# Zero products in TensorE's first gaps, the first pair's squares on one engine, u by tokens in single products, and two heads' sums in one tile, in a fused attention and mixer kernel

## The chip, the cores and the metric

The kernel runs on one core of one Trainium2 chip. The metric is the device time of one execution in microseconds (us), as a median of several executions. Where two kernels are compared, their runs were taken on the same chip in the same rounds.

## The reference, cut to what matters

```python
# q, k, v: (8 batches, 12 heads, 448 tokens, 64); U: (448, 32); V: (32, 448); w_ch1: (768, 3072)
q_n = q / (norm(q) + 1e-6);  k_n = k / (norm(k) + 1e-6)
attn = softmax(q_n @ k_n.T / tau)
x = (attn @ v), heads side by side        # (8, 448, 768)
u = x + (x.T @ U @ V).T                   # low rank, over tokens
out = u + relu(u @ w_ch1) @ w_ch2
```

## The kernel before

The kernel does not leave the order of instructions to the hardware or to luck. Each piece of work is an `Op` with an engine, an assumed duration, dependencies and buffers (`Slot`s of a `Ring`). A planner runs these through a list schedule and then emits them in the order of their planned starts. TensorE has several streams; at any time it takes the first stream whose next product is ready. Below that plan, the framework that the kernel is written in puts in the semaphore waits, that is, the points where one engine waits for another. A tile is a named buffer. PSUM, in the code below, is the memory into which TensorE writes its sums.

The parts that matter here:

```python
r_mm = ring(3, [128, 512], FP, "mm", psum)          # each ring entry is a PSUM tile of its own
r_sc = ring(3, [128, 512], FP, "sc", psum)
r_av = ring(2, [128, 4, D + 8], FP, "av", psum)     # sums of attn @ v, one tile for each of two heads
# ... cut ...
def attention(b, p, X):                              # one pair of heads
    # 7 score products (sc), each followed by one exponential on ScalarE (attn), then for each head
    for t in range(4):
        for j in range(4):                           # 16 products of 65 columns into av
            nc.tensor.matmul(out=av.tile[:, t, 0:D + 1], lhsT=attn..., rhs=v_t..., ...)
    # and on VectorE
    nc.vector.reciprocal(out=rd.tile, in_=av.tile[:, :, D:D + 1])                    # rd <- av
    nc.vector.tensor_mul(X.tile[...], av.tile[:, :, 0:D], rd.tile.to_broadcast(...)) # X_sb <- av, rd
# ... cut ...
def by_tokens(us, A, X):                             # batch 0: u in token order, six products
    for i in range(3):
        for c0, c1 in ((0, CH), (CH, C)):
            ...                                      # one product into mm, one addition on VectorE
# ... cut: in the first mixer product of batch 0 ...
if b == 0 and f == 9:
    by_tokens(us, *state["first"])
```

Of the kernel before, what the change touches and what calls it, by code (L numbers as in the profile page):

```python
# [10 lines left out]
FP = mybir.dt.float32  # L11
# [38 lines left out]
class Plan:  # L50
# [52 lines left out]
    def run(self):  # L103
# [22 lines left out]
        while left:  # L126
            if not events:
                raise RuntimeError("plan stuck")
            t = heapq.heappop(events)
            while events and events[0] <= t + 1e-9:  # L130
                heapq.heappop(events)
            progress = True
            while progress:
                progress = False
                for e in self.ENGINES:
                    if free[e] > t + 1e-9:
                        continue
                    pick = None
                    if e in heads:
                        for k, s in enumerate(self.streams[e]):  # L140
                            i = heads[e][k]
                            if i < len(s):
                                r = self.ready_at(s[i], e)
                                if r is None:
                                    continue
                                if r <= t + 1e-9:
                                    pick = s[i]
                                    heads[e][k] += 1
                                    break
                                heapq.heappush(events, r)  # L150
                    else:
                        w = known[e]
                        for i, (_, _, o) in enumerate(w):
                            if o.start is not None:
                                continue
                            if e == "ACT" and o.fast and free["DVE"] <= t + 1e-9:
                                continue
                            r = self.ready_at(o, e)
                            if r is None:
                                continue  # L160
                            if r <= t + 1e-9:
                                pick = o
                                break
                            heapq.heappush(events, r)
                            if r <= t + self.HOLD:
                                break
                        if pick is not None:
                            del w[i]
                    if pick is None:
                        continue  # L170
                    o = pick
                    o.start, o.by = t, e
                    o.end = t + (o.dur[e] if isinstance(o.dur, dict) else o.dur)
                    free[e] = o.end
                    o.end += self.LAG[e]
                    if isinstance(o.lat, tuple):
                        q, work, fixed = o.lat
                        dma[q] = max(dma[q], o.end) + work
                        o.end = dma[q] + fixed
                    else:  # L180
                        o.end += o.lat
                    for s in o.acq:
                        if s.i is None:
                            s.i = s.ring.n
                            s.ring.n += 1
                    for s in o.rel:
                        s.left -= 1
                        s.last = max(s.last, o.end)
                        if s.left == 0:
                            s.ring.freed[s.i] = s.last  # L190
                    for c in kids.pop(o.seq, ()):
                        waits[c.seq] -= 1
                        if waits[c.seq] == 0:
                            offer(c)
                    order.append(o)
                    left -= 1
                    progress = True
                    heapq.heappush(events, free[e])
                    heapq.heappush(events, o.end + self.SEM)
# [5 lines left out]
def kernel(  # L205
# [12 lines left out]
    nc = tc.nc  # L218
# [13 lines left out]
    EPS = 1e-6  # L232
    PE_BATCHES = 2
    LATE = 8.0

    const = ctx.enter_context(tc.tile_pool(name="const", bufs=1))
    pool = ctx.enter_context(tc.tile_pool(name="pool", bufs=1))
# [9 lines left out]
    def ring(n, shape, dt, name, space=None):  # L247
        p = space or pool
        return Ring(n, lambda i: p.tile(shape, dt, name=name, tag=name, bufs=n))
# [42 lines left out]
    r_rd = ring(2, [128, 4, 1], FP, "rd")  # L292
    r_mm = ring(3, [128, 512], FP, "mm", psum)
    r_sc = ring(3, [128, 512], FP, "sc", psum)
    r_av = ring(2, [128, 4, D + 8], FP, "av", psum)


    U_sb = const.tile([128, 2, 4, R], BF, name="U_sb")
    V_sb = const.tile([128, PAD + S + PAD], BF, name="V_sb")
    ident = const.tile([128, 128], BF, name="ident")  # L300
    w1_sb = const.tile([128, CC, F], BF, name="w1_sb")

    nc.scalar.preload_act_table_set("natural_log_exp_and_others")
# [17 lines left out]
    pe_a = plan.stream("PE")  # L321
    pe_sc = plan.stream("PE")
    pe_mlp = plan.stream("PE")
    pool_q = plan.stream("POOL")

    def pe_t(n):
        return n / 2400.0 + 0.0025
# [167 lines left out]
    def stats_first(ld, ops):  # L495

        inv = Slot(r_inv, 3)
        done, ups = {}, []
        for i in range(2):
            done[i], up = scales(0, 0, 2, ld, ops, 0, (i,), inv, -1 - 0.1 * i, ("DVE", "ACT")[i])  # L500
            ups.append(up)
        return ups + norm(0, 0, ld, 0, inv, 0, done, -1)

# [12 lines left out]
    def norm(b, p, ld, la, inv, a, deps, pr):  # L516
# [29 lines left out]
        if not by_pe:  # L546
            done = [plan.add(Op("SP", 0.1, lambda: nc.sync.dma_start_transpose(
                out=qkT.tile, in_=xn.tile.rearrange("p b e -> p (b e)")), deps=ops, acq=[qkT],
                rel=[xn], prio=0, lat=("x", 0.05 * 84, LATE)))]
        else:  # L550
            done = []
            for b0, b1, o in blocks:
                done.append(flip(
                    pe_tp, [(lambda z=z: xn.tile[:, z, :]) for z in range(b0, b1)], SCH,
                    lambda: qkT.tile, (lambda t_, x, b0=b0, b1=b1: key_tiles(t_, x, b0 // 4, b1 // 4)
                                   if b == 0 and b0 < 8 else [(t_[:, b0:b1, :], x)]),
                    [o], [qkT], [xn], 1, "ACT/DVE", 0.09 if first else 0.05, b == 0 and b0 < 8))
        got[b, p, "qkT"] = (qkT, lambda m: (done[:2] if m < 3 else done) if first else done, done)
        return ops

# [1 line left out]
    def attention(b, p, X):  # L562
# [4 lines left out]
        for m in (0, 1, 2, 6, 3, 4, 5) if b == 0 else range(7):  # L567
            sc = Slot(r_sc, 1)

            def score(sc=sc, m=m):  # L570
# [1 line left out]
                nc.tensor.matmul(out=sc.tile[:, 0:S], lhsT=kT[:, 128 * m:128 * (m + 1)],  # L572
                                 rhs=qkT.tile[:, 8:12, :].rearrange("p c s -> p (c s)"),
                                 start=True, stop=True)
            o = plan.add(Op("PE", 0.31 if b == 0 and p == 0 else pe_t(S), score, deps=qdeps(m), acq=[sc], rel=[qkT]),
                         pe_first if b == 0 else pe_sc)
            exps[m] = plan.add(Op("ACT", act_t(S), lambda sc=sc, m=m: nc.scalar.activation(  # L577
                out=attn.tile[:, m, off:off + S], in_=sc.tile[:, 0:S], func=AF.Exp,
                scale=inv_tau), deps=[o], acq=[attn], rel=[sc], prio=0.1 if b == 0 else 1))
        last_exp[b] = exps[5]  # L580
        muls = []
        for hh in range(2):
            h = 2 * p + hh
# [138 lines left out]
        prev["A"], prev["X"] = A, X  # L722
        return us, uT, ut

    def by_tokens(us, A, X):

        for i in range(3):
            for c0, c1 in ((0, CH), (CH, C)):
                mm = Slot(r_mm, 1)
                o = plan.add(Op("PE", pe_t(CH), lambda i=i, c0=c0, c1=c1, mm=mm: nc.tensor.matmul(  # L730
                    out=mm.tile[:, 0:CH], lhsT=V_sb[:, PAD + 128 * i:PAD + 128 * i + 128],
# [7 lines left out]
    def mlp(b, us, uT, ut):  # L739
# [28 lines left out]
        for f in range(NC):  # L768
            if f % AHEAD == 0:
                for g in range(f, f + AHEAD):  # L770
                    early[g] = Slot(r_sc if b == 0 and f == 0 else r_mm, 1)
                    if f == 0 and b == 0:
                        up(g, early[g], range(CC - 1))
            if b == 0 and f == 9:
                by_tokens(us, *state["first"])
            mm = early[f]
            o = up(f, mm, range(CC - 1, CC) if b == 0 and f < AHEAD else range(CC))
            r = Op("ACT/DVE", any_t(n), None, deps=[o], acq=[relu], rel=[mm],
# [65 lines left out]
        nc.vector.memset(t_[96:128, :, 0:PAD].bitcast(mybir.dt.uint32), ones)  # L844

    attn_set = [fill(lambda t_=t_: set_attn(t_), 1000, prio=i - 2.5) for i, t_ in enumerate(attn_t)]
    z = fill(lambda: nc.vector.memset(V_sb, 0.0), 500, prio=-1.3)

    def load_u(par):
        off = PAD * par  # L850
# [15 lines left out]
                       in_=V_f().rearrange("r (s c) -> r c s", c=SC))  # L866


    w2_ops = []
    NW = 4  # L870
    THIRDS = [(0, 4), (4, 8), (8, 12)]
# [4 lines left out]
    state, last_mul = {}, []  # L876

    def att(b):
        X = Slot(r_X, 0)
        muls = []  # L880
        for p in range(NPAIR):
            muls += attention(b, p, X)
        last_mul.extend(muls)
        return stage0(b, X, muls)
# [2 lines left out]
        out=lead.tile[:, i], in_=src[0, 0:2].rearrange("h (s c) d -> s h (c d)", c=SC)),  # L887
        acq=[uv], prio=-5, lat=2.5)) for i, src in enumerate((q, k))]
    second = load_qk(0, 2, 4, uses=2)
    ld, ops, _ = load_qk(0, 4, 8)  # L890
    id_set = plan.add(Op("POOL", 0.8, lambda: make_identity(nc, ident)), pool_q)
    begun = stats_first(*first[:2])
    stats(0, 2, 4, *second, hold=begun)
    xn_set.append(fill(lambda: nc.vector.memset(xn_t[2][:, 0:8, :], 0.0), 900, prio=0.2, deps=begun))
    zf = fill(lambda: nc.vector.memset(U_f(), 0.0), 400, prio=0.1, acq=[uv], deps=begun)
    u0 = load_u(0)
    v0 = [plan.add(Op("SP", 0.45, lambda t=t: nc.sync.dma_start(out=V_f()[R * t:R * (t + 1)], in_=moe_V),
                      deps=[zf, *begun], prio=-2, lat=12.0)) for t in range(4)]
    u1 = load_u(1)
    stats(0, 4, 8, ld, ops, 0, hold=got[0, 0, "qkT"][2])  # L900
    load_v0()
    ld, ops, _ = load_qk(0, 8, 12)
    late = stats(0, 8, 12, ld, ops, 0)
    load_w1(0, 6)
    load_w1(6, 12)
    v_set = [fill(lambda: set_v(v_t[0]), 1000, prio=-1.4),
             fill(lambda: set_v(v_t[1]), 1000, prio=3, deps=late)]
    consts = [plan.add(Op("POOL", 0.4, lambda: cast_u(0), deps=u0 + [z], rel=[uv]), pool_q),
              plan.add(Op("POOL", 1.2, cast_v, deps=v0 + [z], rel=[uv]), pool_q),
              plan.add(Op("POOL", 0.4, lambda: cast_u(1), deps=u1 + [z], rel=[uv]), pool_q)]  # L910
# [67 lines left out]
```

## Time and profile before

| | before |
|---|---|
| median of three executions | 604.51 us (604.49 to 605.16) |
| span of the profiled run | 603.2 us |
| TensorE busy | 586.4 us, 97% |
| full TensorE clock recorded from | 17.77 us |
| last exponential of batch 0 starts | 37.31 us |

The result below has a fourth execution of this kernel, which moves the median to 604.84.

How to read the lines further down. In the order of instructions, a line gives start, length, engine, source line, operation, output and inputs, shapes, how many were merged, and in brackets the idle time before it with what ended it. The tile names say what the work is: `sc` scores, `attn` their exponentials, `av` products with v, `rd` and `X_sb` VectorE's two steps that empty `av`, `tp` transposes, `warm` the zeros.

### The profile page before, as it was taken

Reading aid. Unit: us, or ns where it says so; the run is one execution under the profiler, and the core shown is the slowest. Engines: PE = TensorE matmul, PEld = TensorE weight load, DVE = VectorE, ACT = ScalarE, POOL = GpSimd, SP = SyncE. Lnnn points to the kernel's source line nnn. Section 1 sums busy time; section 2 is a strip of 40 time slices with the busy share of each in tenths; the row PEclk is TensorE's granted clock in tenths of the full one; section 3 lists DMA queues with packets and bytes.
Section 4 is the critical chain, followed back from the end, with each engine's and each line's share of the span. In section 5 each row is a group of like instructions: output and inputs, shape, how many; then the busy total and the mean of one; then the engine's idle time right before and its main releaser. Section 6 shows DMA issues by size and latency. Waiting matters only on the chain.

```text
span 603.2 us, 11528 instructions
## 1 busy us (share of the span) xinstructions
PE 586.4 (97%) x4725; PEld 347.0 (58%) x4725; DVE 300.6 (50%) x728; ACT 276.9 (46%) x598; POOL 115.2 (19%) x175
## 2 busy tenths in 40 slices
PE   3899999999999999999999999999999999999997
PEld 1565666555565665666445666566545666654565
DVE  8979749989999988554731244014300210110011
ACT  5877652488874277316741067505642025014300
POOL 8246334062706116000600000000000000000000
PEclk9999999999999999999999999999999999999999
DMA  9999999999999959725922133030002110310021
GB/s 144 193 188 112 204 201 107 150 173 136 159 152 155 149 102 154 95 57 90 123 29 66 52 74 47 1 93 27 15 1 53 52 40 1 90 42 1 0 53 54
DMA packets 150165, 54.81 MB, mean 91 GB/s; under 512 B 115040, under 2 KB 150112, under 8 KB 150112
## 3 DMA queue, kind: packets, MB, share of 16 engines
q0 software_dynamic: 72864, 25.73, 38.4%
q1 hardware_dynamic: 77184, 28.32, 24.4%
q8 instruction: 37, 0.61, 0.4%
q14 instruction: 16, 0.13, 0.1%
q10 hardware_dynamic: 64, 0.02, 0.0%
HBM read 52.25 MB, written 11.01 MB: 105 GB/s over the span
## 4 chain that ended last, share of the span: by engine, by line
PE 93%; DVE 2%; ACT 2%; POOL 1%; DMA 1%; issue 0%; ACTq 0%; POOLq 0%
PE mm L794 36%; PE mm L760 35%; PE sc L572 10%; PE av L592 8%; PE mm L684 1%; PE tp L374 1%; DMA v_nat<-in_v_dram 1%; DVE xn L536 1%; PE mm L649 1%; POOL v_nat L429 1%; ACT attn L577 1%; PE sc L760 0%; POOL qk_nat L396 0%; DVE ss L461 0%; ACT qkT L824 0%
## 5 line engine op out<-in xcount | busy, mean ns | idle before, releaser
L760 PE MATMUL mm<-uT,w_sb 128*128 128x512 bf16 (+1 forms) x1134 | 241.3, 353 | 0.2 <-DVE u_nat L734 0.2
L794 PE MATMUL mm<-w_sb,relu 128*128 128x384 bf16 (+1 forms) x1368 | 231.3, 323 | 0.0
L577 ACT ACTIVATE attn<-sc 128x448 bf16<-128x448 f32 x336 | 164.6, 552 | 110.9 <-PE av L592 58.2
L794 PEld LDWEIGHTS <-relu 128*128 128x128 bf16 x1368 | 132.7, 98 | 86.1 <-issue 0.2
L760 PEld LDWEIGHTS <-w_sb 128*128 128x128 bf16 x1152 | 111.8, 98 | 102.7 <-issue 1.8
L783 ACT ACTIVATE relu<-mm 128x512 bf16<-128x512 f32 (+1 forms) x158 | 86.8, 549 | 129.3 <-PE mm L760 128.7
L803 DVE TENSOR_TENSOR O_sb<-mm,u_nat 128x384 f32<-128x384 f32 (+1 forms) x57 | 31.2, 549 | 210.8 <-PE mm L794 207.4
L572 PE MATMUL sc<-qkT 128*128 128x448 bf16 x336 | 102.7, 356 | 3.7 <-ACT attn L577 2.0
L592 PEld LDWEIGHTS <-attn 128*128 128x128 bf16 x1536 | 62.1, 98 | 17.8 <-issue 2.5
L418 POOL DMA_DIRECT2D v_nat<-in_v_dram x98 | 63.2, 655 | 31.7 <-DMA w_sb<-in_moe_w_ch_dram 15.8
L592 PE MATMUL av<-v_nat,attn 128*128 128x65 bf16 x1536 | 66.6, 194 | 0.8 <-DMA v_nat<-in_v_dram 0.4
L461 DVE TENSOR_REDUCE ss<-sq 112x8 f32<-112x512 bf16 x96 | 63.1, 673 | 0.2
L536 DVE TENSOR_TENSOR xn<-qk_nat,inv 112x512 bf16<-112x512 bf16 x94 | 60.9, 681 | 2.4 <-DMA qkT<-xn 2.2
L396 POOL DMA_DIRECT2D qk_nat<-in_q_dram x24 | 17.2, 718 | 136.5 <-DVE xn L536 117.0
L572 PEld LDWEIGHTS <-qkT 128*128 128x128 bf16 x336 | 28.9, 98 | 22.1 <-issue 7.3
L601 DVE TENSOR_TENSOR X_sb<-av,rd 128x256 bf16<-128x256 f32 x96 | 40.1, 419 | 1.6
L599 DVE RECIPROCAL rd<-av 128x4 f32<-128x4 f32 x96 | 17.1, 179 | 37.6 <-PE av L592 36.9
L457 DVE TENSOR_TENSOR sq<-qk_nat 112x512 bf16<-112x512 bf16 x87 | 33.7, 415 | 0.0
L698 DVE TENSOR_TENSOR u_nat<-mm,X_sb 128x384 bf16<-128x384 f32 x36 | 19.2, 553 | 15.4 <-PE mm L684 15.1
L785 DVE TENSOR_SCALAR relu<-mm 128x384 bf16<-128x384 f32 (+1 forms) x31 | 18.7, 604 | 12.8 <-PE mm L760 12.0
L374 PE MATMUL tp<-ident,xn 112*128 112x112 bf16 x144 | 11.9, 226 | 7.8 <-DVE xn L536 7.6
L474 ACT ACTIVATE ln<-ss 112x32 f32<-112x32 f32 (+2 forms) x26 | 6.0, 231 | 27.3 <-DVE ss L461 27.1
(61 smaller groups left out, 172.5 us busy)
## 6 DMA issues: line engine op xcount, KB each, us to landing
qk_nat<-in_q_dram POOLq DMA_DIRECT2D x23, 224.0 KB, 5.2
qk_nat<-in_k_dram POOLq DMA_DIRECT2D x23, 224.0 KB, 6.3
w_sb<-in_moe_w_ch_dram POOLq DMA_DIRECT2D x4, 1152.0 KB, 14.6
w_sb<-in_moe_w_ch_dram POOLq DMA_DIRECT2D x8, 576.0 KB, 15.8
out_dram<-O_sb SPq DMA_DIRECT2D x15, 168.0 KB, 2.2
out_dram<-O_sb SPq DMA_DIRECT2D x16, 144.0 KB, 2.1
out_dram<-O_sb SPq DMA_DIRECT2D x16, 120.0 KB, 2.0
out_dram<-O_sb SPq DMA_DIRECT2D x16, 96.0 KB, 2.2
```

The costliest lines, as they stand in the source:

```text
L418: nc.gpsimd.dma_start(out=vb[p0:p0 + s1 - s0, hs, j, 0:D], in_=v[b, hs].rearrange("h (s c) d -> c s h d", c=SC)[c, s0:s1]),
L457: nc.vector.tensor_mul(y, x, x)
L461: lambda i=i, a0=a0, a1=a1, sq=sq: nc.vector.reduce_sum(ss.tile[:, i, a0:a1, :].rearrange("p h c -> p (h c)"), sq.tile[:, 0:a1 - a0, :].re ...
L536: nc.vector.tensor_mul(dst, src, sc)
L572: nc.tensor.matmul(out=sc.tile[:, 0:S], lhsT=kT[:, 128 * m:128 * (m + 1)], rhs=qkT.tile[:, 8:12, :].rearrange("p c s -> p (c s)"), start=T ...
L577: exps[m] = plan.add(Op("ACT", act_t(S), lambda sc=sc, m=m: nc.scalar.activation(out=attn.tile[:, m, off:off + S], in_=sc.tile[:, 0:S], fu ...
L592: nc.tensor.matmul(out=av.tile[:, t, 0:D + 1], lhsT=attn.tile[:, m, 128 * t:128 * (t + 1)], rhs=v_t[b % 2][:, h, j, 0:D + 1], start=(j == ...
L601: muls.append(plan.add(Op("DVE", dve_t(256), lambda av=av, rd=rd, h=h: nc.vector.tensor_mul(X.tile[:, :, h * D:(h + 1) * D], av.tile[:, :, ...
L760: o = plan.add(Op("PE", pe_t(n), lambda cc=cc: nc.tensor.matmul(out=mm.tile[:, 0:n], lhsT=w1_sb[:, cc, f * 128:(f + 1) * 128], rhs=uT.tile ...
L783: nc.scalar.activation(out=relu.tile[:, f, 0:n], in_=mm.tile[:, 0:n], func=AF.Relu)
L794: nc.tensor.matmul(out=mm.tile[:, 0:c1 - c0], lhsT=relu.tile[:, f, i * 128:(i + 1) * 128], rhs=w2_t[:, f, c0:c1], start=(f == 0), stop=(f ...
L803: nc.vector.tensor_add(out=O.tile[:, 0:w], in0=mm.tile[:, 0:w], in1=us[i].tile[:, c0:c1]),
```

## The change

The intent has three parts. TensorE is to run products of zeros in the gaps that the plan leaves up to the second pair of heads, so that its clock is full when real work comes (before, the full clock is recorded only from 17.77 us). The squares of the first pair's q and k go to ScalarE alone. The six "u by tokens" products, which stood in a block, go one by one between the long products. For the zeros, the change needs a place in PSUM that nobody reads, and takes it from the `av` banks. To have a name for that place, it puts both heads' sums into one tile; `fixed_ring` hands out its two halves in turn.

```diff
@@ the planner: ScalarE leaves quick work to a free VectorE only if VectorE may do it
-                            if e == "ACT" and o.fast and free["DVE"] <= t + 1e-9:
+                            if e == "ACT" and o.fast and "/" in o.eng and free["DVE"] <= t + 1e-9:
@@
+    WARM = 150
-    r_av = ring(2, [128, 4, D + 8], FP, "av", psum)
+    av_t = psum.tile([128, 2, 512], FP, name="av", tag="av", bufs=1)
+    r_av = fixed_ring([av_t[:, i, 0:4 * (D + 8)].rearrange("p (t d) -> p t d", t=4) for i in range(2)])
+    warm = const.tile([128, 208], BF, name="warm")
@@ squares of the first pair
-            done[i], up = scales(0, 0, 2, ld, ops, 0, (i,), inv, -1 - 0.1 * i, ("DVE", "ACT")[i])
+            done[i], up = scales(0, 0, 2, ld, ops, 0, (i,), inv, -1 - 0.1 * i, "ACT")
@@ u by tokens
-            if b == 0 and f == 9:
-                by_tokens(us, *state["first"])
+            if b == 0 and 9 <= f < 21 and f % 2:
+                by_tokens(us, *state["first"], (f - 9) // 2)
@@ the zeros: a stream of TensorE with the lowest rank
+    warm_set = fill(lambda: nc.vector.memset(warm, 0.0), 100, prio=-9)
+    for i in range(WARM):
+        plan.add(Op("PE", pe_t(208), lambda i=i: nc.tensor.matmul(
+            out=av_t[:, 1, 304:512], lhsT=warm[:, 0:128], rhs=warm, start=(i == 0), stop=True,
+            skip_group_check=True), deps=[warm_set]), pe_warm)
@@ ... cut: assumed durations at the start, the order in which loads and squares of batch 0 are set up ...
```

More of the change, by code (lines that the diff above doesn't have):

```diff
@@ L323 @@
     pe_mlp = plan.stream("PE")
+    pe_warm = plan.stream("PE")
     pool_q = plan.stream("POOL")
@@ L556, in norm @@
                                    if b == 0 and b0 < 8 else [(t_[:, b0:b1, :], x)]),
-                    [o], [qkT], [xn], 1, "ACT/DVE", 0.09 if first else 0.05, b == 0 and b0 < 8))
+                    [o], [qkT], [xn], 1, "ACT/DVE", 0.05, b == 0 and b0 < 8))
         got[b, p, "qkT"] = (qkT, lambda m: (done[:2] if m < 3 else done) if first else done, done)
@@ L574, in score @@
                                  start=True, stop=True)
-            o = plan.add(Op("PE", 0.31 if b == 0 and p == 0 else pe_t(S), score, deps=qdeps(m), acq=[sc], rel=[qkT]),
+            o = plan.add(Op("PE", pe_t(S), score, deps=qdeps(m), acq=[sc], rel=[qkT]),
                          pe_first if b == 0 else pe_sc)
@@ L580, in attention @@
         last_exp[b] = exps[5]
+        if b == 0 and p == 0:
+            last_exp["first"] = [exps[1]]
         muls = []
@@ L723, in stage0, with by_tokens @@
         return us, uT, ut
-    def by_tokens(us, A, X):
-        for i in range(3):
-            for c0, c1 in ((0, CH), (CH, C)):
+    def by_tokens(us, A, X, part):
+        for i in range(part // 2, part // 2 + 1):
+            for c0, c1 in [((0, CH), (CH, C))[part % 2]]:
                 mm = Slot(r_mm, 1)
@@ L846 @@
     attn_set = [fill(lambda t_=t_: set_attn(t_), 1000, prio=i - 2.5) for i, t_ in enumerate(attn_t)]
-    z = fill(lambda: nc.vector.memset(V_sb, 0.0), 500, prio=-1.3)
     def load_u(par):
@@ L878, in att @@
     def att(b):
-        X = Slot(r_X, 0)
-        muls = []
-        for p in range(NPAIR):
+        X = Slot(r_X, 0) if b else X0
+        muls = [] if b else list(muls0)
+        for p in range(0 if b else 1, NPAIR):
             muls += attention(b, p, X)
@@ L889 @@
     second = load_qk(0, 2, 4, uses=2)
-    ld, ops, _ = load_qk(0, 4, 8)
+    third = load_qk(0, 4, 8)
     id_set = plan.add(Op("POOL", 0.8, lambda: make_identity(nc, ident)), pool_q)
-    begun = stats_first(*first[:2])
+    load_v0()
+    fourth = load_qk(0, 8, 12)
+    v_set = [fill(lambda: set_v(v_t[0]), 1000, prio=-1.4)]
+    begun = stats_first(*first)
+    X0 = Slot(r_X, 0)
+    muls0 = attention(0, 0, X0)
     stats(0, 2, 4, *second, hold=begun)
     xn_set.append(fill(lambda: nc.vector.memset(xn_t[2][:, 0:8, :], 0.0), 900, prio=0.2, deps=begun))
+    z = fill(lambda: nc.vector.memset(V_sb, 0.0), 500, prio=3, deps=begun)
     zf = fill(lambda: nc.vector.memset(U_f(), 0.0), 400, prio=0.1, acq=[uv], deps=begun)
@@ L899 @@
     u1 = load_u(1)
-    stats(0, 4, 8, ld, ops, 0, hold=got[0, 0, "qkT"][2])
-    load_v0()
-    ld, ops, _ = load_qk(0, 8, 12)
-    late = stats(0, 8, 12, ld, ops, 0)
+    stats(0, 4, 8, *third, hold=last_exp["first"])
+    late = stats(0, 8, 12, *fourth)
     load_w1(0, 6)
     load_w1(6, 12)
-    v_set = [fill(lambda: set_v(v_t[0]), 1000, prio=-1.4),
-             fill(lambda: set_v(v_t[1]), 1000, prio=3, deps=late)]
+    v_set.append(fill(lambda: set_v(v_t[1]), 1000, prio=3, deps=late))
     consts = [plan.add(Op("POOL", 0.4, lambda: cast_u(0), deps=u0 + [z], rel=[uv]), pool_q),
```

## The prediction

> **What bounds the kernel now.** I read the page first, then the busy time by stretches, then the order of instructions on TensorE and ScalarE in the first 60 us, and last the chain that ended last.
>
> ```profile
> PE 586.4 (97%) x4725; PEld 347.0 (58%) x4725; DVE 300.6 (50%) x728; ACT 276.9 (46%) x598; POOL 115.2 (19%) x175
> PE   3899999999999999999999999999999999999997
> PEclk9999999999999999999999999999999999999999
> ```
>
> TensorE is busy for 97% of the span, and only the first two slices and the last one (15 us each) are not full. So the time is TensorE's products plus what is lost at the start, plus small losses. The busy time by stretches says the same:
>
> ```profile
> 0.00:7.60 7.60, 0.00 (x0) 1.00 0.80 132
> 7.60:14.33 6.73, 4.92 (x22) 1.00 2.01 152
> 14.33:17.77 3.44, 3.23 (x43) 1.00 1.26 179
> 17.77:30.00 12.23, 9.75 (x113) 1.00 1.14 198
> 30.00:41.29 11.29, 10.88 (x171) 1.00 1.18 178
> 41.29:50.00 8.71, 8.71 (x62) 1.00 1.40 182
> 50.00:54.00 4.00, 3.23 (x22) 1.00 0.68 43
> 54.00:603.20 549.20, 545.73 (x4298) 1.00 0.57 84
> ```
>
> (Columns: stretch, its length, busy us, instructions, clock, DMA share, GB/s.) After 54 us nothing is to be had but the closing 3.2 us, which the change does not touch. The gaps are at 0 to 41 and, small, at 50 to 54. "Busy" flatters TensorE, since a product counts until its end though the next one may start earlier. By start-to-start distances at full speed (products of 384 columns follow each other at 0.1625 us in the long rows[...]) the products in each stretch need less. Set against that, 21.2 us are lost before 41.29 and 1.5 us between 50 and 54. These two sums are my own, from the trace's single records.
>
> The clock row shows 9 everywhere, yet the distances show a slow start:
>
> ```profile
> 7.62 1.55 PE L374 MATMUL tp<-ident,xn 112*128 112x112 bf16 x12 [7.62 <-DVE xn L536]
> 9.42 1.30 PE L572 MATMUL sc<-qkT 128*128 128x448 bf16 x3 [0.26 <-ACT qkT L824]
> 14.33 1.25 PE L592 MATMUL av<-v_nat,attn 128*128 128x65 bf16 x15 [0.44 <-DMA v_nat<-in_v_dram]
> 15.39 0.94 PE L374 MATMUL tp<-ident,xn 112*128 112x112 bf16 x8
> 17.65 0.77 PE L572 MATMUL sc<-qkT 128*128 128x448 bf16 x3
> 19.79 0.56 PE L374 MATMUL tp<-ident,xn 112*128 112x112 bf16 x8
> ```
>
> Eight transposes take 0.94 us at 15.39 and 0.56 us at 19.79. From start to start that is 93 ns against 49 ns in the single records. The trace's record of the granted full clock begins at 17.77 us. So the first 17.8 us run at half speed, and the page's clock row does not show it.
>
> Half speed is not what carries this stretch, though. The chain that ended last has a load in it, and ScalarE after it:
>
> ```profile
> 9.48 5.13 DMA v_nat<-in_v_dram
> 14.65 0.93 PE av L592 x14
> 17.06 0.53 ACT qkT L824
> ```
>
> The first pair's products with v wait for v until 14.65. The second pair's transposes stand behind them in TensorE's order, its key and query copies follow, and its first score product comes at 17.65, its first exponential at 18.14. From there ScalarE is nearly gapless until 32 us (one exponential each 0.424 us), with only 1.75 us of gaps up to the last exponential of batch 0 at 37.31. The chain to the first long products (41.29) hangs on that one.
>
> The loss at 50 to 54 us is the six "u by tokens" products in one block:
>
> ```profile
> 50.01 1.17 PE L730 MATMUL mm<-A_sb,V_sb 128*128 128x384 bf16 x3
> 52.39 0.79 PE L730 MATMUL mm<-A_sb,V_sb 128*128 128x384 bf16 x2 [0.24 <-DVE u_nat L734]
> 53.39 0.33 PE L730 MATMUL mm<-A_sb,V_sb 128*128 128x384 bf16 x1
> ```
>
> There are three PSUM buffers for them, and each is freed by a VectorE addition that stands behind reductions and squares of the next batch.
>
> [...] The zero products write unread columns of a bank that the second head's sums use, but in the new order VectorE reads that bank only after the last of them was due. [...] I count it as no cost in time.
>
> **The change, part by part.**
>
> *Zero products.* There are 150 of 208 columns. The new order on TensorE is: 72 of them; the 12 transposes of pair 0 with 7 between; 13; 3 scores; 9, 3, 5 and 5 each followed by one score; 14; then 17 products with v, the second pair's 8 transposes, 7 with v, 4 transposes, 8 with v, 12 zero products; the second pair's first 3 scores; 10 more later. The planner counts 0.0892 us each and fills every gap, so TensorE in the plan has no slack from about 1.15 us on (the zero tile is set by a memset of some 0.15 us that starts at 0.92). Up to the second pair's first score: 140 x 0.0892 = 12.49, 24 transposes x 0.049 = 1.18, 7 scores x 0.189 = 1.32, 32 products with v x 0.030 = 0.95. With 1.15 that makes 17.1 us, against 17.65 before. This holds only at full clock from the first product. [...] TensorE works in order and its plan is packed, so the delay is carried on: pair 0's transposes at about 9.6 (7.62 before), its first score near 12 (9.42), the second pair's first score near 19.2 (17.65) and its first exponential near 19.5 (18.14). What is gained at full clock (some 1 us between 14.65 and 17.06) is already in this count.
>
> *What ScalarE does with it.* From the second pair's first exponential to the start of the last one, before: 34 x 0.424 = 14.42, one square 0.52, copies 1.31 + 0.90, four small ones' 0.24: 17.4, plus 1.75 of gaps. In the new order: the same exponentials and square, three copies of keys at 0.90 in place of those 2.21, 0.24: 17.9. The later start leaves VectorE time to have scales and xn ready, so the gap of 0.70 at 26.2 should go, and the 1.0 at 32 to 37 (TensorE behind) shrink to perhaps 0.4. So the last exponential starts at about 19.5 + 17.9 + 0.4 = 37.8 instead of 37.3: +0.5 us, give or take 0.9. After it TensorE is full, so this goes to the end one for one.
>
> *First pair's squares both on ScalarE.* Before, VectorE squared one (0.62 us, 4.34) beside ScalarE's other (0.63 us). Now they are one after the other, 0.52 apart, but VectorE's two reductions (0.64 apart) were in series anyway. Cost near 0, and in any case hidden behind the 72 zero products.
>
> *u by tokens, one at a time.* Each product now stands before every second block of six long ones, so an addition has some 2 us to free its buffer while two others turn. Of the 1.5 us lost at 50 to 54 I expect 1.2 back.
>
> Sum: 604.5 + 0.5 - 1.2 = 603.8. As a change kept by someone who tunes this kernel is more likely to help than not, I lean a little lower: 603.5.
>
> **Rivals.** (1) *The warm-up wins*: the delay of the cold zero products is absorbed since ScalarE has squares and copies to do in the meantime, and the last exponential comes 1 us earlier; with the 1.2 us that gives about 602.3. For it: the half clock until 17.77 is real. Against it: ScalarE, not TensorE's speed, sets 18 to 32. (2) *The zero products are in the way*: clock late (6 us or more), no gap of ScalarE closes; +2 us at the start, -1 at the tokens: 605.5. For it: no slack in the plan. (3) *The additions only move the wait*: VectorE is busy 9 of 10 us from 40 to 60, a held buffer delays the relu products instead, and the 1.2 us become 0.3: 604.7.
>
> **Range and chances.** The mechanical terms are +0.5 (0.9 either way) and -1.2 (0.5 either way); with run-to-run differences of 0.7 between the three times before, 602.0 to 605.2 should hold it 8 times in 10. Two per cent is 12 us, more than half of all that is lost before 41 us, so "within 2%" is nearly sure.
>
> **What would show it.** Zero products 173 ns apart at first, then 89 ns, the full clock between 3.5 and 7.5 us; the first transpose at 9 to 10.5; the second pair's first score at 18.3 to 20; the last exponential of batch 0 at 37 to 38.7; no wait on u_nat at 50 to 54. Wrong would be: a second pair that starts before 17.6 (the delay was absorbed), a last exponential before 36.5, or new losses after 54 us.

Passages that said of the hardware what no trace of this case shows are cut where marked, and with them a term of the sum. The 17.1 us up to the second pair's first score count the zero products at full clock from the first one. A cut passage put 2.1 us of delay on that, for the first ones running at half speed: the author's estimate, since the trace of the kernel before shows that its first 17.77 us run at half speed, and not what ends it. So 17.1 + 2.1 = 19.2 us; the other times of the new order (9.6, 12, 19.5) and the 3.5 to 7.5 us for the full clock rest on that estimate too. The rest of the sum stands as it was: the last exponential at 37.8 against 37.31, which is +0.5, less 1.2 for the token products, 604.5 + 0.5 - 1.2 = 603.8, leaned to 603.5.

## More of the kernel before

In the waits, a line gives who waited for whom, the sum in us, how often, and the longest. Lines that are left out between two shown ones are marked by three dots.

## The result, and the profile after

| | before | after |
|---|---|---|
| median | 604.84 us (604.49 to 605.16) | 620.88 us (619.65 to 621.01) |
| ratio | | 1.0261 (95%: 1.0243 to 1.0279) |
| span of the profiled run | 603.2 us | 619.2 us |

A ratio is the mean time of one kernel's fast runs over that of the other's fast runs of the same rounds, so it is not quite the ratio of the medians.

The change made the kernel 2.6% slower; 603.5 us had been predicted. The first place to look is the start. This is the order on TensorE in the changed kernel, first 20 us:

```profile
1.03 9.09 PE L876 MATMUL av<-warm 128*128 128x208 bf16 x72 [1.03 <-DVE warm L874]
9.96 0.36 PE L378 MATMUL tp<-ident,xn 112*128 112x112 bf16 x4
...
12.35 0.73 PE L576 MATMUL sc<-qkT 128*128 128x448 bf16 x3
...
19.56 0.73 PE L576 MATMUL sc<-qkT 128*128 128x448 bf16 x3
```

Up to here it went as predicted. The zero products started 0.173 us apart until the full clock was recorded at 6.2 us, and 0.089 us apart from then on. The transposes began at 9.96 (predicted 9.6), the second pair's scores at 19.56 (predicted 19.2), and its first exponential at 19.95 (predicted 19.5). By stretches (same columns as in the prediction), the losses come later:

```profile
17.77:30.00 12.23, 9.88 (x131) 1.00 1.19 205
30.00:48.88 18.88, 14.59 (x201) 1.00 1.29 183
48.88:57.50 8.62, 8.62 (x62) 1.00 1.09 92
57.50:62.00 4.50, 4.20 (x33) 1.00 1.09 164
62.00:619.20 557.20, 547.20 (x4288) 1.00 0.55 80
```

Of 18.88 us from 30 on, TensorE is busy for 14.59. Before, the stretch from 30 to the same point of the program was 11.29 us with 10.88 busy. After 62 us, 10.0 us are idle, where the closing 3.2 explain only a part; before, 3.5 us after 54 had been all. The last product with v of a batch shows how the loss builds up (single records of the traces, each the start of the batch's last such product; the third column of times is experiment e1 below):

| last product with v starts | before | after | e1 |
|---|---|---|---|
| batch 0 | 38.4 | 46.0 | 40.0 |
| batch 3 | 181.5 | 191.2 | 181.1 |
| batch 5 | 291.8 | 305.4 | 292.3 |
| batch 7 | 432.9 | 449.0 | 433.5 |

So some 6 us more than e1 are lost in batch 0, and 9.5 more in small pieces until batch 7. TensorE's waits in the changed kernel name the piece:

```profile
PE av L598 <- DVE X_sb L607: 7.4, 15, 0.8
PE av L598 <- DVE rd L605: 3.0, 11, 0.3
```

Before, the only wait of `av` in that list was one for a load, and the weight loads in front of these products waited for `X_sb` twice, 0.7 us in all:

```profile
PE av L592 <- DMA v_nat<-in_v_dram: 0.4, 1, 0.4
```

A look at the order of instructions on three engines in the changed kernel shows how such a wait comes about:

```profile
33.10 0.42 DVE L607 TENSOR_TENSOR X_sb<-av,rd 128x256 bf16<-128x256 f32 x1 [0.20 <-PE av L598]
33.58 0.25 PE L598 MATMUL av<-v_nat,attn 128*128 128x65 bf16 x3 [0.33 <-DVE X_sb L607]
...
34.37 0.42 DVE L607 TENSOR_TENSOR X_sb<-av,rd 128x256 bf16<-128x256 f32 x1 [0.31 <-PE av L598]
34.84 0.19 PE L598 MATMUL av<-v_nat,attn 128*128 128x65 bf16 x1 [0.52 <-DVE X_sb L607]
...
37.48 0.54 ACT L581 ACTIVATE attn<-sc 128x448 bf16<-128x448 f32 x1 [1.67 <-PE sc L576]
```

TensorE and VectorE take turns. `X_sb` ends at 33.52, then three products run. VectorE waits for products, reads, and TensorE waits for that reading before it may do a single further product at 34.84. The score products stand behind in TensorE's order, and ScalarE, which had been nearly gapless in this stretch before, waits 1.67 us for one. In the same stretch of the kernel before, `X_sb` empties one buffer from 33.73 to 34.15 while TensorE goes on and fills the other from 33.94:

```profile
33.50 0.42 PE L592 MATMUL av<-v_nat,attn 128*128 128x65 bf16 x8
...
33.73 0.42 DVE L601 TENSOR_TENSOR X_sb<-av,rd 128x256 bf16<-128x256 f32 x1
33.75 0.35 PE L572 MATMUL sc<-qkT 128*128 128x448 bf16 x1
33.94 0.41 PE L592 MATMUL av<-v_nat,attn 128*128 128x65 bf16 x8
```

In the changed kernel the two buffers act as one.

The built programs (the instructions with their semaphore waits that come out of kernel.py) say why. No time is in this, only what waits for what:

```
                                              before   after   e1 (two tiles)
products with v, or their weight loads,
  with a semaphore wait for VectorE               52      89               52
X_sb that waits for TensorE by itself              0      19                0
```

The two heads' sums are two halves of one tile, and the framework orders accesses by tile, although the halves lie in different banks (0 and 1, where the built e1 has its two tiles) and no column is shared. A filling waits for the last reading of the other half, and a reading for products that were issued into the other half before it. All 89 waits of the changed program are of this kind (68 for an `X_sb`, 21 for an `rd`, each of the other half), and so are the 19; before and in e1, every one of the 52 is for the reading of the buffer that is to be filled again. Writing the tile flat as 1024 columns instead of 2 x 512 left the built counts (89 and 19) as they were.

### The profile page after: what moved, and what is told of

The parts are those of the page before. It is cut to its first block, busy times and chain, and to the rows that moved or that the text cites. A ratio compares the mean times of both kernels' runs of the same rounds, so it can differ in the third digit from the quotient of the medians.

```text
span 619.2 us, 11854 instructions
## 1 busy us (share of the span) xinstructions
PE 601.2 (97%) x4875; PEld 361.1 (58%) x4875; DVE 304.5 (49%) x730; ACT 278.3 (45%) x597; POOL 114.2 (18%) x175
## 4 chain that ended last, share of the span: by engine, by line
PE 90%; DVE 8%; ACT 1%; issue 1%; ACTq 0%
PE mm L800 33%; PE mm L766 33%; PE sc L576 9%; PE av L598 8%; PE av L876 2%; DVE ss L465 2%; DVE xn L540 2%; PE mm L690 1%; DVE X_sb L607 1%; DVE sq L461 1%; PE mm L655 1%; DVE O_sb L809 1%; DVE rd L605 1%; PE tp L378 1%; ACT attn L581 1%
## 5 line engine op out<-in xcount | busy, mean ns | idle before, releaser
L789 ACT ACTIVATE relu<-mm 128x512 bf16<-128x512 f32 (+1 forms) x155 | 84.9, 548 | 131.5 <-PE mm L766 130.8
L576 PE MATMUL sc<-qkT 128*128 128x448 bf16 x336 | 101.0, 352 | 1.9 <-ACT attn L581 1.7
L598 PE MATMUL av<-v_nat,attn 128*128 128x65 bf16 x1536 | 68.1, 193 | 10.6 <-DVE X_sb L607 7.4
L791 DVE TENSOR_SCALAR relu<-mm 128x384 bf16<-128x384 f32 (+1 forms) x34 | 20.7, 607 | 11.7 <-PE mm L766 10.9
L876 PE MATMUL av<-warm 128*128 128x208 bf16 x150 | 17.8, 277 | 1.0 <-DVE warm L874 1.0
## 6 DMA issues: line engine op xcount, KB each, us to landing
w_sb<-in_moe_w_ch_dram POOLq DMA_DIRECT2D x8, 576.0 KB, 15.5
```

The source lines that it names most:

```text
L576: nc.tensor.matmul(out=sc.tile[:, 0:S], lhsT=kT[:, 128 * m:128 * (m + 1)], rhs=qkT.tile[:, 8:12, :].rearrange("p c s -> p (c s)"), start=T ...
L598: nc.tensor.matmul(out=av.tile[:, t, 0:D + 1], lhsT=attn.tile[:, m, 128 * t:128 * (t + 1)], rhs=v_t[b % 2][:, h, j, 0:D + 1], start=(j == ...
L789: nc.scalar.activation(out=relu.tile[:, f, 0:n], in_=mm.tile[:, 0:n], func=AF.Relu)
```

## The experiments

**e1: the changed kernel, sums in two tiles.** All else as changed.

```diff
-    av_t = psum.tile([128, 2, 512], FP, name="av", tag="av", bufs=1)
-    r_av = fixed_ring([av_t[:, i, 0:4 * (D + 8)].rearrange("p (t d) -> p t d", t=4) for i in range(2)])
+    av_t = [psum.tile([128, 512], FP, name=f"av{i}", tag=f"av{i}", bufs=1) for i in range(2)]
+    r_av = fixed_ring([av_t[i][:, 0:4 * (D + 8)].rearrange("p (t d) -> p t d", t=4) for i in range(2)])
...
-            out=av_t[:, 1, 304:512], lhsT=warm[:, 0:128], rhs=warm, start=(i == 0), stop=True,
+            out=av_t[1][:, 304:512], lhsT=warm[:, 0:128], rhs=warm, start=(i == 0), stop=True,
```

> The changed kernel with the sums of the two heads (av) in two PSUM tiles of one bank each, as before the change, instead of one tile of two banks; zero products, squares and u by tokens as changed. Theory (one tile is one thing to wait for: a head's products wait for VectorE's reading of the other head's sums): the whole loss goes, 603 to 605 us, the wait of av for X_sb falls from 7.4 us to under 1.5, and pair 1's first score stays near 19.6. Rival A (the zero products, carried on through TensorE's order, are the loss): at least 615. Rival B (VectorE has more squares and copies at the start): at least 615.

Measured: 605.48 us median against 605.59 of before, ratio 0.9996 (0.9984 to 1.0009). The whole loss is gone. In the built programs the two tiles lie in the same two banks as the two halves did, so the place in PSUM is not the cause. TensorE's wait in e1:

```profile
PE av L598 <- DVE X_sb L607: 0.2, 1, 0.2
```

It was 7.4 us in 15 waits. The second pair's first exponential is at 19.54, nearly as late as in the changed kernel (19.95; 18.14 before), so the delayed start is not the loss. Rivals A and B fall: the zeros and the squares are all still there.

**e2: the kernel before, sums in one tile.** The opposite test.

```diff
-    r_av = ring(2, [128, 4, D + 8], FP, "av", psum)
+    av_t = psum.tile([128, 2, 512], FP, name="av", tag="av", bufs=1)
+    r_av = fixed_ring([av_t[:, i, 0:4 * (D + 8)].rearrange("p (t d) -> p t d", t=4) for i in range(2)])
```

> The kernel before with nothing changed but the sums of both heads in one PSUM tile of two banks. Theory (one tile is one thing to wait for): 618 to 623 us, with av waiting for X_sb some 7 us and waits for the sequencer before it of some 15. Rivals A and B: unchanged, 604 to 605.5, since there are no zero products and the order of the engines is that of before.

Measured: 623.31 us median, ratio 1.0288 (1.0273 to 1.0302), just above what was expected (618 to 623). These two lines alone make the old kernel slower by about as much as the whole change did (1.0261; the intervals just overlap). They also replace the ring that makes new tiles by one over fixed tiles; e1 and e6 have that ring too and lose nothing. TensorE's waits in e2:

```profile
PE av L593 <- DVE X_sb L602: 9.7, 19, 0.9
...
PE av L593 <- DVE rd L600: 2.5, 9, 0.3
```

**e3: e1 without the zeros.**

```diff
-    WARM = 150
+    WARM = 0
```

> e1 without the 150 zero products (number set to 0). If zero products delay the second pair by some 1.5 us and ScalarE makes up most of it, as predicted: 0.5 us faster than e1 (about 603.3). If warming up pays (rival 1 of the prediction): 1 us or more slower than e1. The full clock should then come at 16 to 20 us instead of 6.2.

Measured: 605.60 us median (604.78 to 606.77), ratio to before 0.9996 (0.9984 to 1.0009), the same as e1. So with two tiles the zeros neither gain nor cost, as far as these intervals (0.8 us either way) can tell; both expectations miss, the first by the half microsecond that five rounds hardly resolve. The trace's record of the full clock began only at 28.2 us, later than the 16 to 20 that I expected. That is the profiled run, the slowest of the five; the fastest (604.78) shows a mean clock of 0.991, so its clock took another course. In the profiled run the first transposes came at 6.98 instead of e1's 9.54, but the second pair's first exponential at 20.03 instead of 19.54. What the zeros take at the start and what half speed takes later would, by these four starts, be about equal; that is an estimate.

**e4: e1 with u by tokens in a block again.**

```diff
-            if b == 0 and 9 <= f < 21 and f % 2:
-                by_tokens(us, *state["first"], (f - 9) // 2)
+            if b == 0 and f == 9:
+                for part in range(6):
+                    by_tokens(us, *state["first"], part)
```

> e1 with the six products of u by tokens in one block again, as before the change. As predicted: 1.2 us slower than e1, with the u_nat wait of TensorE back near 57 us. If the wait only moves when they are spread (rival 3 of the prediction): within 0.4 us of e1.

Measured: 607.01 us median, ratio to before 1.0024 (1.0011 to 1.0038): 1.5 us slower than e1, and the intervals do not overlap. The order on TensorE in e4 has the old picture back (predicted near 57 us; it is near 53, since that was counted from the slower kernel):

```profile
51.09 1.17 PE L736 MATMUL mm<-A_sb,V_sb 128*128 128x384 bf16 x3
...
53.47 0.79 PE L736 MATMUL mm<-A_sb,V_sb 128*128 128x384 bf16 x2 [0.24 <-DVE u_nat L740]
```

**e5: the kernel before with single token products alone.** If e4 is right, this part needs no other.

```diff
-    def by_tokens(us, A, X):
-        for i in range(3):
-            for c0, c1 in ((0, CH), (CH, C)):
+    def by_tokens(us, A, X, part):
+        for i in range(part // 2, part // 2 + 1):
+            for c0, c1 in [((0, CH), (CH, C))[part % 2]]:
...
-            if b == 0 and f == 9:
-                by_tokens(us, *state["first"])
+            if b == 0 and 9 <= f < 21 and f % 2:
+                by_tokens(us, *state["first"], (f - 9) // 2)
```

> The kernel before with one part of the change: u by tokens one product at a time. e4 against e1 gave 1.5 us for it in the changed order. Theory (that gain stands by itself, and the rest of the change, with two tiles, costs the same 1.5): 1.2 to 1.6 us faster than before, some 0.9975 of it. Rival (in the old order the additions only move the wait): within 0.4 us of before.

Measured: 604.36 us median against 605.83, ratio 0.9977 (0.9963 to 0.9991): 1.4 us faster, as expected. Two of the eleven runs of the kernel before (607.16 and 606.83) show a mean clock of 0.997, the other nine 0.999 or 1.000. Without these two the gain is 1.2 us. On this evidence it beats both the kernel before and the changed one, and it is the smallest of the changes tried. The order on TensorE in e5 at the first of the six:

```profile
51.10 0.32 PE L730 MATMUL mm<-A_sb,V_sb 128*128 128x384 bf16 x1
51.55 0.48 PE L760 MATMUL mm<-uT,w_sb 128*128 128x384 bf16 x2
```

Long products follow 0.45 us later; the next token product comes at 55.67, when the addition (51.48 to 52.03) has long freed its buffer. No wait for `u_nat` is left in TensorE's list.

**e6: e5 with 34 zeros at the very start.** They are planned at their cold duration (0.1735 us; the changed kernel's first ones started 0.173 us apart), and `av` is in two tiles as in e1.

```diff
+    WARM = 34
+    warm_set = fill(lambda: nc.vector.memset(warm, 0.0), 100, prio=-9)
+    for i in range(WARM):
+        plan.add(Op("PE", 0.1735, lambda i=i: nc.tensor.matmul(
+            out=av_t[1][:, 304:512], lhsT=warm[:, 0:128], rhs=warm, start=(i == 0), stop=True,
+            skip_group_check=True), deps=[warm_set]), pe_warm)
```

> e5 plus 34 zero products at the very start only, which the planner counts at the cold 0.1735 us, so that they end near 7 us, before the first transposes; sums in two tiles. If the half clock until 17.8 costs about 1 us on the way to the second pair: 0.5 to 1 us faster than e5, full clock at 4.5 to 8 us. If ScalarE hides it: within 0.3 us of e5. If the clock falls back in the gaps after the zeros: a second half-clock stretch in the trace and no gain.

Measured: 604.45 us median, ratio 0.9978 (0.9963 to 0.9993), the same as e5. The third expectation came true. By stretches, e6:

```profile
0.00:7.00 7.00, 5.97 (x34) 1.00 0.78 132
7.00:10.50 3.50, 1.93 (x16) 0.99 1.99 160
10.50:20.70 10.20, 7.64 (x55) 0.50 1.42 167
```

Up to 7 us the 34 zeros took 5.97 us, 0.176 us each, about the 0.173 of the changed kernel's first ones; the clock column reads 1.00 there all the same, as it did in the slow start of the kernel before. From 7.00 to 10.50 us the mean clock was 0.99, and from 10.50 to 20.70 it was 0.50: the clock fell back to half at about 10.5 us. The changed kernel, with zeros in the later gaps too, has full clock recorded from 6.2 us to the end of its span.

**e7: e1 with the first 30 zeros planned at their cold duration.**

```diff
-        plan.add(Op("PE", pe_t(208), lambda i=i: nc.tensor.matmul(
+        plan.add(Op("PE", 0.1735 if i < 30 else pe_t(208), lambda i=i: nc.tensor.matmul(
```

> e1 with the first 30 of the 150 zero products planned at 0.1735 us, what they take at half clock, so that only 44 stand before the first transposes instead of 72. If the carried delay of 2 us (first transposes at 9.6 instead of 7.6) is what the start of e1 loses: first transposes near 7.8, second pair's exponentials at about 17.8 instead of 19.5, 1 to 1.7 us faster than e1. If ScalarE and VectorE set the start anyway: within 0.4 us of e1.

Measured: 604.71 us median, ratio 0.9981 (0.9968 to 0.9993). Against e1's 0.9996, taken in other rounds, this is some 0.9 us faster (0.7 without the two runs named under e5); the two intervals overlap, so it is likely and not sure. It lies between the two expectations (1 to 1.7 us, or within 0.4). It is no better than e5, though it has everything: the token products, a full clock recorded from 4.78 us (its first 44 zeros took 5.90 us, where 44 at 0.173 would take 7.6) and first transposes at 7.00. Its order on TensorE shows what the clock cannot buy:

```profile
12.33 1.77 PE L876 MATMUL av<-warm 128*128 128x208 bf16 x18
13.93 0.23 PE L598 MATMUL av<-v_nat,attn 128*128 128x65 bf16 x2
14.99 0.20 PE L598 MATMUL av<-v_nat,attn 128*128 128x65 bf16 x1 [0.84 <-DMA v_nat<-in_v_dram]
```

TensorE is early and then waits for v. The products with v get going only at 15.36, and the second pair's first exponential is at 18.82. The gain of 2.5 us at the first transposes has shrunk to 0.7 us (19.54 to 18.82).

**e8: the changed kernel, one tile, no zeros.**

```diff
-    WARM = 150
+    WARM = 0
```

> The changed kernel, sums in one tile, with no zero products. Theory (the tile alone is the loss, as e2 says, and the zeros have no part in it): 618 to 623 us. Rival (zeros written into the shared tile are what makes the waits): 604 to 607.

Measured: 618.48 us median, ratio 1.0212 (1.0193 to 1.0230). The waits are there with no zeros in the tile (`av` for `X_sb`: 6.1 us in 14 waits), so the shared tile alone makes them. It is some 3 us less than the changed kernel's 1.0261, with intervals that do not overlap. At the last exponential of batch 0 the two are equal (43.94 and 43.88), so the 3 us arise later, when all zeros are long done. The orders differ in places, and the built program has 85 waits of products with v for VectorE where the changed one has 89; which place it is was not tried.

## Why the prediction was wrong

**The step that failed** is in the list of parts. I listed zero products, squares and token products, and what ScalarE does with the start. The replacement of two PSUM tiles by one had no item and no time. The only sentence near it, "I count it as no cost in time", was about where in PSUM the zeros are written, and that part held: the last zero product started at 21.12, VectorE first read that bank at 26.67, and e1, with the zeros in the same columns, came out at 0.9996 of before. The cost was in the program instead: one tile is one thing to wait for. That "within 2%" was nearly sure rested on the same list of parts. e1 takes the 2.6% away by two tiles, e2 puts 2.9% on the old kernel by one tile, e8 shows it without zeros. As to the size: in the single records, pauses before a product with v (over 0.25 us from start to start, less 0.17) add up to 12.9 us in the changed kernel and to 1.1 us in e1. That is 11.8 of the 15.5 us between the two spans. The rest I take to be what follows from these pauses on other engines; that was not itemised and is not shown.

**"After it TensorE is full, so this goes to the end one for one"** fell with it. TensorE's order interleaves products with v of later batches with long products, and a wait of one holds up what stands behind it: in the stretch above it waited 0.52 us at 34.84 and 0.51 at 37.02, and the score product behind the second wait started at 37.09, after which ScalarE's wait of 1.67 us ended. The text had named "new losses after 54 us" as a sign that it was wrong, and they came. The built program already showed the 89 waits before any run; I had read its order, and not its waits.

**The zero products** were right in their mechanics: cold at first (0.173 us apart), full clock at 6.2 us (3.5 to 7.5 predicted) and 0.089 us apart after it, first transposes at 9.96, the second pair 1.8 us later than before (1.4 in e1, as predicted). Their worth was near nil (e1 and e3 are equal), so rival 1, that warming up wins, fell. Rival 2 was right in its parts (in e1 the last exponential is at 38.91 against 37.31, and ScalarE's gaps stayed) and fell in its sum: with two tiles there is no loss of 1 us. Its reason, the packed plan, holds in e7, where a plan with the cold durations starts the transposes 2.5 us earlier. What the prediction said against rival 1 was that ScalarE sets the pace; e7 adds that the arrival of v does, before that.

**ScalarE's stretch.** Predicted were 18.3 us from the second pair's first exponential to the last (17.9 of work and 0.4 of gaps). In e1, where the tile does not disturb, it took 38.91 - 19.54 = 19.4 us, as long as before (19.2). The work was the 17.9 us; the gaps, 1.75 us before, were still 1.5 us and did not close. That term was mis-sized by 1.1 us.

**The squares** were given no cost. No run changes them alone, so that is left open; e1 bounds what they and the zeros do together with the new order at the start. By e4 that sum is about 1.4 us (607.01 against 605.59), which the token products give back. Since e1 and e3 put the zeros near nil, the squares or the new order may cost that; no run parts the two.

**The token products** were right: 1.2 us predicted, 1.5 measured in the changed order (e4 against e1), 1.4 in the old one (e5). Rival 3, that the wait only moves, fell. Had the tile been left alone, the sum would have been 603.8 against 604.5; e1 came out at the same time as before, 0.6 us off: the ScalarE term, less what the token products gave above their 1.2. The lean from 603.8 to 603.5 had no reading of the profile behind it.

**A sum to correct.** The 21.2 us that the prediction has as lost before 41.29 are 20.2 in a recount by its own rule. Nothing rests on the difference.

## What to carry to other kernels

Where waits are put in by tile, as in this kernel's framework, two buffers in one tile act as one, which here cost 2.9% (e2): allocate each half of a double buffer as its own tile, and when only a name for spare columns is needed, take it from one of them. Before running a change that touches a buffer's allocation, count the waits between producer and consumer in the built program, old against new. Before warming a clock, look at what the stretch waits for; here it was a load and ScalarE, and 150 extra products gained nothing that five rounds could resolve (e1 and e3, both at 0.9996 of before).
